# Local attention and a bilinear GLU in one kernel: products over finished q, k rows, tile sums on ScalarE

## The chip, the cores and the metric

The kernel runs on one core of a Trainium2 chip. The metric is the device time of one execution in microseconds (us); smaller is better. A core has a matrix engine (TensorE, PE in the profile), a vector engine (VectorE, DVE), a scalar engine (ScalarE, ACT), a general engine (GpSimd, POOL), a queue engine that here only starts transfers (SyncE, SP), and 16 DMA engines that move the data. Each engine takes its own instructions strictly in order; they meet through semaphores.

## The reference

```python
x = A_x                                   # 1 x 2048 x 640, bf16
xn = layernorm(x)                         # (x - mean) / sqrt(var + 1e-5)
q, k, v = split(xn @ wqkv)                # 32 heads of 20
idx = pos[:, None] - arange(8) * 2        # 8 window positions, 2 apart, back in time
logits = einsum("bhsd,bhswd->bhsw", q, k[idx]) * 20 ** -0.5     # idx < 0: -1e9
o = einsum("bhsw,bhswd->bhsd", softmax(logits), v[idx])
h = (xn @ w_gate) * (xn @ w_up)           # 640 -> 1536; the input B_x is not used
out = x + o @ wo + h @ w_down
```

The two branches read the same normalized xn, and their sum is added to x.

## The kernel before

The 2048 positions are 16 tiles of 128 (`t`), in four chunks of 512 (`c`, tiles 4c to 4c+3). A chunk goes through these stages:

- **Layer norm** (`ln`), by tile, on x with positions on partitions. For every tile DVE takes `bn_stats` of two halves (L251), aggregates (L257) and adds epsilon (L259); POOL raises to -1/2 (`rstd`, L265). Tiles 0-7 are then applied by DVE (L270); for tiles 8-15 POOL makes a shift (`ns`, L312) and ACT applies (L315).
- **Transposes** into `xnT` (channels on partitions): by PE for tiles 0-3, by DMA transposes on SP's queue for the others (L353). `xnT` has two buffers, one a chunk.
- **q, k, v** by PE (`qk` L419, `vproj` L452) into a ring of six PSUM banks; ACT copies every result out (L426, L458). POOL's queue stores v to DRAM (`vD`, L473), and SP loads it back as a window of eight shifted copies for each tile (`load_v8`, L613, 1280 KB).
- **Logits** (`products`, `fold`, `logits`). With channels on partitions, DVE multiplies q by shifted k (L520): eight instructions a chunk, each for two window positions and half a chunk, in five blocks of channels (`KT` = 5). Four tiles `("pw", c, u)` hold them. `fold` adds blocks together (L496); `LEVELS` says how far: chunk 0 leaves three blocks, chunk 1 two, chunks 2 and 3 one. PE sums over channels with a 0/1 matrix `Ek` (L539), four matmuls for each block that is left, in two groups `g` a chunk. ACT copies the logits out (L555), a DMA transpose on SP makes positions partitions (LT, L562).
- **Softmax** on DVE in two blocks for each half chunk (`mx` L581-585, `nrm` L598-603), Exp on ACT between them (L590).
- **Attention** (`av`), by tile: DVE multiplies the window by the weights (L638), adds up in a tree (L647, L651, L653) to `o`; SP transposes o to `oT` (L660, four buffers).
- **GLU** (`glu`): PE in 24 groups a chunk (L680), ACT copies out (L685), DVE multiplies to `hT` (L696).
- **Down** (`down`): for each tile PE sums hT by w_down (L740) and oT by wo (L743); ACT copies to `y` (L755); POOL's queue adds y to the output in DRAM (L784), which was seeded with x. The last two tiles go by DVE and SP.

One pool tag `pv` with five buffers holds both the products' tiles and the window loads, so that a window load can wait for PE's logits, and a product for an attention tile.

The order of the work on every engine is made by a planner in the kernel (`Plan`): every step has an engine, a cost, an occupation and dependencies; it is emitted by its planned start, the most urgent first. Emission order is the order on each engine. The planner knows the dependencies that are given to `add`; a buffer's reuse that isn't given is still waited for on the chip. An ACT or DVE step that follows another of its own engine is taken as ready when that one's occupation ends. The logits are urgent in PE's order (`LL[n].urgent`), and take a margin. `ring` gives the PSUM banks: a PE group waits for the copy that is six groups back.

Of the kernel before, what the change touches and what calls it, by code (L numbers as in the profile page):

```python
# [31 lines left out]
class Plan:  # L32


    LAG = 0.06
    INORDER = ("DVE", "PE", "ACT")
# [4 lines left out]
    def add(self, eng, cost, fn, deps=(), occ=None, after=(), kb=0):  # L41
        s = Step(eng, cost, fn, deps, occ, after)
        s.kb = kb
        s.idx = len(self.steps)
        self.steps.append(s)
        return s

    def order(self):
# [16 lines left out]
        while True:  # L65
            best = None
            for eng, items in ready.items():
                if not items:
                    continue
                f = free.get(eng, 0.0)  # L70
                t0 = max(f, min(r for r, _ in items))
                r, s = min((x for x in items if x[0] <= t0 + 1e-9), key=lambda x: (x[1].late, x[1].idx))
                if best is None or t0 < best[0]:
                    best = (t0, r, s)
# [10 lines left out]
            for t in s.succ:  # L85
                t.left -= 1
                if t.left == 0:
                    at = max(
                        d.start + d.occ if d in t.after else (d.start + d.occ if d.eng == t.eng and d.eng in self.INORDER else d.end + (0.0 if d.eng == t.eng else self.LAG) + t.margin)
                        for d in t.deps  # L90
                    )
                    ready.setdefault(t.eng, []).append((at, t))
# [5 lines left out]
def kernel(  # L98
# [17 lines left out]
    H = 32  # L116
# [182 lines left out]

    def ln(t):  # L300
        turn = [XT.get(t - (1 if t == CH else 2)), GL.get(t - 1)] if t < 2 * CH else []
        a = add("DVE", 0.48, ln_stats(t, 0), [X[t], GL.get(t - 3), *turn], occ=0.395)
        a = add("DVE", 0.48, ln_stats(t, 1), [a], occ=0.395)
        a = GL[t] = add("DVE", 0.39, ln_aggr(t), [a], occ=0.3)
        b = RS[t] = add("POOL", 0.56, ln_rstd(t), [a])
# [4 lines left out]
        def shift():  # L310
            ns = new(("ns", t), [P, 1], F32, "ns", 6)
            nc.gpsimd.tensor_scalar(ns[:], T["mv", t][:, 0:1], scalar1=T["rstd", t][:], scalar2=-1.0, op0=ALU.mult, op1=ALU.mult)  # L312
# [82 lines left out]
    Q, Kk, LASTPW = {}, {}, {}  # L395
    HALOCP = {}

    def halo(c):
# [8 lines left out]
        else:  # L407
            HALOCP[c] = add("ACT", 0.25, fn, [LASTPW.get(c - 2), *Kk[c - 1]])

    def qk(c, lo, n, rs=(0, 1)):  # L410
        for r in rs:
            for j in range(KT):
# [17 lines left out]
                mine = [WK if r else WQ, *[TX.get(t, TT[t]) for t in ts], LASTPW.get(c - 2)]  # L430
# [50 lines left out]
    PW, LL, LE, SS, DD, AA, O16, OE, V8, DT = {}, {}, {}, {}, {}, {}, {}, {}, {}, {}  # L481

    LEVELS = (1, 2, 3, 3)
    FOLDER = ('DVE', 'DVE', 'DVE', 'DVE')
    LEFT = (tuple(range(KT)), (0, 1, KT - 1), (0, KT - 1), (0,))
    HALVES = ((0, 2, 2, 4), (0, 1, 1, 2), (0, 1, KT - 1, KT))

    HS = CS // 2

    def fold(c, u):  # L490
        s = PW[8 * c + 2 * u + 1]
        for lo, hi, a, b in HALVES[: LEVELS[c]]:
            def fn(lo=lo, hi=hi, a=a, b=b):
                w = T["pw", c, u]
                if FOLDER[c] == "DVE":
                    nc.vector.tensor_tensor(w[:, :, lo:hi, :], w[:, :, lo:hi, :], w[:, :, a:b, :], ALU.add)  # L496
                else:
                    nc.gpsimd.dma_start(out=w[:, :, lo:hi, :], in_=w[:, :, a:b, :], accum_op=ALU.add)
            n = (hi - lo) * 4 * HS
            if FOLDER[c] == "DVE":  # L500
                s = add("DVE", 0.25 + n / 1920, fn, [s], occ=0.1 + n / 1920)
            else:
                s = add("POOL", 6.2, fn, [s], occ=1.2)
        return s

    def products(c, hf):
        for j in range(4):
# [15 lines left out]
            w = [LL.get(2 * c - 1), O16.get(4 * c - 4), O16.get(4 * c - 3), O16.get(4 * c - 2)][u]  # L523
            PW[m] = add("DVE", 1.48, mul, [*Q[c], *Kk[c], w], occ=1.395, after=[(FO[4 * c + 1] if i == 4 else PW.get(m - 1)) if i else V8.get(4 * c - 1)])
            if j % 2:
                FO[4 * c + u] = fold(c, u)
        LASTPW[c] = PW[m]

    PAIRED = ()

    def logits(c, g):
        n = 2 * c + g

        def lg():
            l = new(("lps", c, g), [P, 512], F32, "pl", 2, psum)
            left = LEFT[LEVELS[c]]
            for i in left:
                for j in range(4):
                    nc.tensor.matmul(l[H * j : H * (j + 1), :], lhsT=Ek[:], rhs=T["pw", c, 2 * g + j // 2][:, 2 * (j % 2) : 2 * (j % 2) + 2, i, :],  # L539
                                     start=(i == left[0]), stop=(i == left[-1]), tile_position=(0, H * j),  # L540
                                     skip_group_check=True)

        alone = not (g and c in PAIRED)
        took = 0.022 + 0.2195 * len(LEFT[LEVELS[c]]) + (0.19 if alone else 0.0)
# [30 lines left out]
    def softmax(c, hf):  # L575
        n = 2 * c + hf

        def mx():
            L4 = T["LT", n]
            m = sb.tile([P, 2, 4, H], BF, name="m", tag="m", bufs=1)  # L580
            nc.vector.tensor_tensor(m[:], L4[:, :, 0:4, :], L4[:, :, 4:8, :], ALU.max)  # L581
            nc.vector.tensor_tensor(m[:, :, 0:2, :], m[:, :, 0:2, :], m[:, :, 2:4, :], ALU.max)
            nc.vector.tensor_tensor(m[:, :, 0:1, :], m[:, :, 0:1, :], m[:, :, 1:2, :], ALU.max)
            d = new(("d", n), [P, 2, W, H], F32, "d", 2)
            nc.vector.tensor_tensor(d[:], L4[:], m[:, :, 0:1, :].to_broadcast([P, 2, W, H]), ALU.subtract)

        DD[n] = add("DVE", 1.52, mx, [SS[n], AA.get(n - 2)], occ=1.43)
# [7 lines left out]
        def nrm():  # L595
            d = T["d", n]
            s = sb.tile([P, 2, 4, H], F32, name="s", tag="s", bufs=1)
            nc.vector.tensor_tensor(s[:], d[:, :, 0:4, :], d[:, :, 4:8, :], ALU.add)  # L598
            nc.vector.tensor_tensor(s[:, :, 0:2, :], s[:, :, 0:2, :], s[:, :, 2:4, :], ALU.add)
            nc.vector.tensor_tensor(s[:, :, 0:1, :], s[:, :, 0:1, :], s[:, :, 1:2, :], ALU.add)  # L600
            nc.vector.reciprocal(s[:, :, 0, :], s[:, :, 0, :])
            a = new(("a", n), [P, 2, W, H], BF, "a", 2)
            nc.vector.tensor_tensor(a[:], d[:], s[:, :, 0:1, :].to_broadcast([P, 2, W, H]), ALU.mult)

        AA[n] = add("DVE", 2.33, nrm, [e, O16.get(2 * n - 3)], occ=2.24)

    def load_v8(t):
        def fn():
            v = new(("v8", t), [P, W, D], BF, "pv", 5)
# [21 lines left out]
    def av(t):  # L631
# [17 lines left out]
        def tree2():  # L649
            v = T["v8", t]  # L650
            nc.vector.tensor_tensor(v[:, 0:2, :], v[:, 0:2, :], v[:, 2:4, :], ALU.add)  # L651
            o = new(("o", t), [P, D], BF, "o", 2)
# [5 lines left out]
        def tr():  # L658
            o = new(("oT", t), [P, KT, P], BF, "oT", 4)
            nc.sync.dma_start_transpose(out=o[:], in_=T["o", t][:])  # L660
# [249 lines left out]
```

## Time and profile before

| | us |
|---|---|
| three runs: median (lowest, highest) | 261.53 (261.37, 263.31) |
| the profiled execution | 261.25 |
| its span, first to last instruction | 259.5 |
| busy: PE, DVE, ACT, POOL | 252.8, 230.4, 121.7, 48.5 |

The span is shorter than the time by what lies before the first and after the last instruction. The granted clock of the matrix engine is 1.00 throughout. DVE begins chunk 0's products at 23.2 us, and PE is at chunk 0's GLU from 42 to 68, at its down projections to 87, at chunk 2's q, k, v to 104, chunk 1's GLU to 131, its down projections to 149, chunk 3's q, k, v to 167, chunk 2's GLU to 193 and so on. In the answers about single instructions, a line has its start, the time it took (for `xN`, N instructions merged), engine, line of the kernel, operation, out<-in, shapes, and in brackets how long the engine idled before it and what released it. For transfers the time is that of the issue; the time to landing stands in a list of its own.

### The profile page before, as it was taken

To read this page: it belongs to the slowest core of one execution; us is meant where nothing else is said; L and a number is where in the kernel's file an instruction comes from. 1 tells how busy PE (TensorE), PEld (TensorE's weight loads), DVE (VectorE), ACT (ScalarE), POOL (GpSimd) and SP (SyncE) were. 2 spreads that over 40 slices of the span, in tenths; PEclk is the share of its full clock that TensorE was granted. 3 is DMA by queue.
4 is the path that set the end of the run, shared out by engine and by line. 5 is a ranking of instruction groups with operands and counts; after the bars stand their busy time and mean duration, and the time that the engine had idled before them with its cause. 6 is when DMAs were issued, how large, how long until landed. Compare 5 with 4: busy or idle time off the path is not lost.

```text
span 259.5 us, 3922 instructions
## 1 busy us (share of the span) xinstructions
PE 252.8 (97%) x1451; PEld 141.7 (55%) x1470; DVE 230.4 (89%) x336; ACT 121.7 (47%) x233; POOL 48.5 (19%) x85
## 2 busy tenths in 40 slices
PE   7999999999999999999999989999999999999995
PEld 2655554444676646444467745644457754445763
DVE  5684998999999999799999995999999976999961
ACT  2757566856321457675521156465541136654100
POOL 4552004201042115800222110200031120000110
PEclk9999999999999999999999999999999999999999
DMA  7989994999989604991168925971157236951251
GB/s 219 344 176 237 399 376 125 418 334 247 294 161 254 109 20 130 361 265 27 25 150 155 206 34 155 371 240 25 25 144 207 31 31 148 370 177 24 28 78 51
DMA packets 51507, 46.54 MB, mean 179 GB/s; under 512 B 24626, under 2 KB 49472, under 8 KB 51424
## 3 DMA queue, kind: packets, MB, share of 16 engines
q1 hardware_dynamic: 46704, 37.10, 49.9%
q0 software_dynamic: 3184, 8.05, 15.2%
q10 hardware_dynamic: 1600, 1.15, 1.4%
q8 instruction: 11, 0.18, 0.3%
q14 instruction: 8, 0.07, 0.1%
HBM read 35.39 MB, written 7.55 MB: 165 GB/s over the span
## 4 chain that ended last, share of the span: by engine, by line
PE 54%; DVE 39%; issue 2%; POOL 2%; DMA 1%; ACT 1%; DVEq 0%; ACTq 0%; POOLq 0%
PE ps L680 20%; PE ps L419 11%; PE ps L740 10%; DVE pv L520 9%; DVE pv L638 7%; PE ps L452 6%; DVE pv L496 6%; PE ps L743 4%; DVE pv L647 4%; DVE hT L696 3%; DVE pv L651 2%; PE ps L242 2%; POOL ns L312 1%; DVE st L251 1%; DMA LT<-L 1%
## 5 line engine op out<-in xcount | busy, mean ns | idle before, releaser
L680 PE MATMUL ps<-xnT,wg 128*128 128x512 bf16 x230 | 59.1, 379 | 0.9 <-ACT v_t L458 0.4
L680 PE MATMUL ps<-xnT,wu 128*128 128x512 bf16 x238 | 59.5, 379 | 0.1
L740 PE MATMUL ps<-wd,hT 128*128 128x320 bf16 (+2 forms) x383 | 57.3, 299 | 0.1
L520 DVE TENSOR_TENSOR pv<-q,k 128x2560 bf16<-128x2560 bf16 x32 | 46.0, 1485 | 3.4 <-ACT k L426 3.4
L740 PEld LDWEIGHTS <-hT 128*128 128x128 bf16 x384 | 37.2, 98 | 15.8
L638 DVE TENSOR_TENSOR pv<-pv,a 128x5120 bf16<-128x5120 bf16 x16 | 45.1, 2819 | 0.1
L680 PEld LDWEIGHTS <-wu 128*128 128x128 bf16 x240 | 23.5, 98 | 28.3
L680 PEld LDWEIGHTS <-wg 128*128 128x128 bf16 x240 | 23.2, 98 | 28.7 <-issue 1.6
L685 ACT CAST us<-ps 128x512 bf16<-128x512 f32 x48 | 28.3, 590 | 18.1 <-PE ps L680 17.1
L685 ACT CAST gs<-ps 128x512 bf16<-128x512 f32 x48 | 28.3, 589 | 17.9 <-PE ps L680 17.8
L755 ACT COPY y<-ps 128x320 f32<-128x320 f32 x28 | 11.5, 426 | 53.0 <-PE ps L743 32.5
L496 DVE TENSOR_TENSOR pv<-pv 128x1024 bf16<-128x1024 bf16 (+1 forms) x36 | 31.7, 922 | 0.3
L743 PE MATMUL ps<-wo,oT 128*128 128x320 bf16 (+2 forms) x160 | 27.0, 299 | 0.3 <-DMA oT<-o 0.3
L784 POOL DMA_DIRECT2D out_dram<-y x14 | 12.3, 878 | 78.6 <-ACT y L755 78.6
L647 DVE TENSOR_TENSOR pv<-pv 128x2560 bf16<-128x2560 bf16 x16 | 23.8, 1486 | 0.1
L452 PE MATMUL ps<-wv,xnT 128*128 128x320 bf16 x160 | 23.3, 300 | 0.4 <-ACT xnT L365 0.4
L696 DVE TENSOR_TENSOR hT<-gs,us 128x512 bf16<-128x512 bf16 x48 | 19.6, 418 | 3.8 <-ACT us L685 3.8
L419 PE MATMUL ps<-xnT,wk 128*128 128x512 bf16 x98 | 22.6, 380 | 0.1
L419 PE MATMUL ps<-xnT,wq 128*128 128x512 bf16 x96 | 22.2, 379 | 0.2
L452 PEld LDWEIGHTS <-xnT 128*128 128x128 bf16 x160 | 15.3, 98 | 7.4 <-ACT xnT L365 0.6
L743 PEld LDWEIGHTS <-oT 128*128 128x128 bf16 x160 | 15.4, 98 | 6.9 <-DMA oT<-o 0.7
L419 PEld LDWEIGHTS <-wk 128*128 128x128 bf16 x100 | 11.5, 118 | 10.3 <-issue 1.1
(60 smaller groups left out, 198.2 us busy)
## 6 DMA issues: line engine op xcount, KB each, us to landing
pv<-vD SPq DMA_DIRECT2D x16, 1280.0 KB, 9.1
vD<-v_t POOLq DMA_DIRECT2D x16, 160.0 KB, 5.2
out_dram<-y POOLq DMA_DIRECT2D x14, 160.0 KB, 3.8
wg<-in_B_w_gate_dram SPq DMA_DIRECT2D x1, 1920.0 KB, 7.7
wu<-in_B_w_up_dram SPq DMA_DIRECT2D x1, 1920.0 KB, 12.0
wd<-in_B_w_down_dram SPq DMA_DIRECT2D x1, 1920.0 KB, 12.3
out_dram<-in_A_x_dram POOLq DMA_DIRECT2D x3, 640.0 KB, 6.5
x<-in_A_x_dram SPq DMA_DIRECT2D x11, 160.0 KB, 5.7
```

What stands on the lines that cost most here:

```text
L419: nc.tensor.matmul(T[key][:, 0:n], lhsT=(wk if r else wq)[:, i, :].rearrange("p (c b) -> p c b", b=KT)[:, :, j], rhs=T["xnT", c][:, i, lo ...
L452: nc.tensor.matmul(T["psv", t, n][:, 0:NS], lhsT=T["xnT", c][:, i, q * P : (q + 1) * P], rhs=wv[:, i, n * NS : (n + 1) * NS], start=(i == ...
L496: nc.vector.tensor_tensor(w[:, :, lo:hi, :], w[:, :, lo:hi, :], w[:, :, a:b, :], ALU.add)
L520: nc.vector.tensor_tensor(o, qh, kh, ALU.mult)
L638: nc.vector.tensor_tensor(v[:].rearrange("p w (j h) -> p w j h", j=Dh, h=H), v[:].rearrange("p w (j h) -> p w j h", j=Dh, h=H), T["a", n][ ...
L647: nc.vector.tensor_tensor(v[:, 0:4, :], v[:, 0:4, :], v[:, 4:8, :], ALU.add)
L680: nc.tensor.matmul(ps[:], lhsT=(wu if r else wg)[:, i, f * P : (f + 1) * P], rhs=T["xnT", c][:, i, :], start=(i == 0), stop=(i == KT - 1))
L685: nc.scalar.copy(s[:], T[key][:])
L696: nc.vector.tensor_tensor(h[:], T["gs", c, f][:], T["us", c, f][:], ALU.mult)
L740: nc.tensor.matmul(ps, lhsT=T["hT", c, f][:, q * P : (q + 1) * P], rhs=wd[:, f, sl], start=(f == 0), stop=(f == FT - 1 and not wo_part))
L743: nc.tensor.matmul(ps, lhsT=T["oT", t][:, g, :], rhs=wo[:, g, sl], start=False, stop=(g == KT - 1 and f1 == FT))
L784: nc.gpsimd.dma_start(out=out_flat[t * P : (t + 1) * P, :], in_=T["y", t][:], accum_op=ALU.add)
```

## The change

1. **Products.** Chunk 0 is folded one level and leaves three blocks, as before. Chunks 1-3 are folded three levels to one block (`LEVELS` 1, 2, 3, 3 becomes in effect 1, 3, 3, 3); the last fold writes over rows 0-3 of `k` or `q` of that half chunk, whose products are then done, so that the `pw` tile is free for the next products. `pw` gets two buffers of its own and the window loads three (`v8`); chunk 0's second half borrows two of these. A product in chunks 1-3 waits for the fold two tiles back, and no more for logits or attention.
2. **Softmax** steps are planned one instruction at a time, and the last tree step of attention too; `o` is a step of its own. The planner adds 0.116 us between dependent DVE steps, and lets a more urgent step that is ready within 0.12 us go ahead of a long one.
3. **Layer norm of tiles 8-15**: ACT sums x (Identity with an accumulator), POOL scales to minus the mean (`nm`), ACT sums the squares of x + nm, POOL makes variance plus epsilon (`ve`), `rstd` and the shift (`ns`), and ACT applies as before. Three ACT passes a tile in place of one, four POOL operations in place of two, none on DVE.
4. **Logits** of chunks 2 and 3 are given as a pair: both groups wait for all four folds. Margins are 0.9 for chunk 0 and 2 for the others.
5. **Window loads** wait for the attention tile three back, and a chunk's first for the oT transpose before it. `oT` goes from four buffers to three.

The core of the diff:

```diff
@@ ln @@
+    ST_ACT = (8, 9, 10, 11, 12, 13, 14, 15)
+    def ln_sum(t):
+            nc.scalar.activation(T["x", t][:], T["x", t][:], ACT.Identity, accum_out=sm[:])
+    def ln_mean(t):
+            nc.gpsimd.tensor_scalar(nm[:], T["sm", t][:], scalar1=-1.0 / D, scalar2=None, op0=ALU.mult)
+    def ln_square(t):
+            nc.scalar.activation(sq[:], T["x", t][:], ACT.Square, bias=T["nm", t][:], accum_out=ss[:])
+    def ln_rstd_sq(t):
+            nc.gpsimd.tensor_scalar(ve[:], T["ss", t][:], scalar1=1.0 / D, scalar2=EPS, op0=ALU.mult, op1=ALU.add)
+            nc.gpsimd.tensor_tensor(rs[:], ve[:], mhalf[:], ALU.pow)
...
+        if t in ST_ACT:
+            a = GL[t] = add("ACT", 0.8, ln_sum(t), [X[t]], occ=0.7)
+            a = add("POOL", 0.3, ln_mean(t), [a])
+            a = add("ACT", 0.8, ln_square(t), [a], occ=0.7)
+            b = RS[t] = add("POOL", 0.9, ln_rstd_sq(t), [a])
...
+                nc.gpsimd.tensor_tensor(ns[:], T["nm", t][:], T["rstd", t][:], ALU.mult)
@@ fold, products @@
+    FIRST = 1
+    def summed(c, u):
+        if c == 0:
+            return [T["pw", 0, u][:, :, i, :] for i in LEFT]
+        lo = (u // 2) * HS
+        return [T["k" if u % 2 == 0 else "q", c][:, 0:4, lo : lo + HS]]
...
+        def last():
+            w = T["pw", c, u]
+            nc.vector.tensor_tensor(summed(c, u)[0], w[:, :, 0, :], w[:, :, KT - 1, :], ALU.add)
+        s = add("DVE", 1.22, level(0, 2, 2, 4), [s], occ=1.14)
+        if c == 0 and FIRST == 1:
+            return s
+        s = add("DVE", 0.69, level(0, 1, 1, 2), [s], occ=0.61)
+        if c == 0:
+            return s
+        return add("DVE", 0.69, last, [s, PW[8 * c + 4 * (u // 2) + 3]], occ=0.61)
...
-                    new(("pw", c, u), [P, 4, KT, HS], BF, "pv", 5)
+                    new(("pw", c, u), [P, 4, KT, HS], BF, *(("v8", 3) if c == 0 and hf else ("pw", 2)))
...
-            w = [LL.get(2 * c - 1), O16.get(4 * c - 4), O16.get(4 * c - 3), O16.get(4 * c - 2)][u]
+            w = None if c == 0 else LL[0] if c == 1 and hf == 0 else FO[4 * c + u - 2]
...
-    PAIRED = ()
+    PAIRED = (2, 3)
-        LL[n].margin = 0.9 if alone else 0.0
+        LL[n].margin = (0.9 if c == 0 else 2) if alone else 0.0
@@ load_v8 @@
-            v = new(("v8", t), [P, W, D], BF, "pv", 5)
+            v = new(("v8", t), [P, W, D], BF, "v8", 3)
...
-        order = [SPLAST[0]] if t < CH - 1 else [SS[2 * (t // CH) + 1]] if t % CH in (1, 2) else []
-        c, u = divmod(t, CH)
-        order.append(V8[t - 1] if u else PW[8 * c + 6])
+        order = [SPLAST[0]] if t < CH - 1 else []
+        if t:
+            order.append(V8[t - 1])
+        else:
+            order.append(PW[6])
...
+        if t >= CH and t % CH == 0:
+            order.append(OE[t - 1])
-        w = LL[2 * c + (u - 1) // 2] if u else O16.get(t - 1)
+        w = LL[1] if t in (1, 2) else O16.get(t - 3)
@@ av @@
-            o = new(("oT", t), [P, KT, P], BF, "oT", 4)
+            o = new(("oT", t), [P, KT, P], BF, "oT", 3)
-        O16[t] = add("DVE", 1.35, tree2, [b, OE.get(t - 2)], occ=1.26)
-        OE[t] = add("SP", 2.8, tr, [O16[t], DT.get(t - 4)], occ=1.3, kb=200, after=[V8[2]])
+        b = add("DVE", 0.82, tree2, [b], occ=0.74)
+        O16[t] = add("DVE", 0.49, tree3, [b, OE.get(t - 2)], occ=0.41)
+        OE[t] = add("SP", 2.8, tr, [O16[t], DT.get(t - 3)], occ=1.3, kb=200, after=[V8[2]])
```

`DT[t]` is PE's down projection of tile t. `attention(c)` is built before `down` of the same chunk, so that `DT.get(7 - 3)` finds nothing when the step of tile 7's transpose is built.

Not shown: the planner's two small rules and the softmax steps, which run the same operations as before, one to a step. In SP's built order, chunk 1's three oT transposes of tiles 5-7 now stand ahead of the window loads of tiles 8-10, and these ahead of the four xnT transposes of tiles 12-15.

More of the change, by code (lines that the diff above doesn't have):

```diff
@@ L46, in add, with after_end @@
         return s
+    def after_end(self, d, t):
+        if d in t.after:
+            return d.start + d.occ
+        if d.eng == t.eng and d.eng in self.INORDER:
+            return d.start + d.occ + (self.RAW if d.eng == "DVE" else 0.0)
+        return d.end + (0.0 if d.eng == t.eng else self.LAG) + t.margin
     def order(self):
@@ L72, in order @@
                 r, s = min((x for x in items if x[0] <= t0 + 1e-9), key=lambda x: (x[1].late, x[1].idx))
+                if eng == "DVE" and s.occ > 0.6:
+                    near = min((x for x in items if x[0] <= t0 + 0.12), key=lambda x: (x[1].late, x[1].idx))
+                    if near[1] is not s:
+                        r, s = near
+                        t0 = max(f, r)
                 if best is None or t0 < best[0]:
@@ L87, in order @@
                 if t.left == 0:
[L88 to L91, printed above, removed]
+                    at = max(self.after_end(d, t) for d in t.deps)
                     ready.setdefault(t.eng, []).append((at, t))
@@ L522, in products @@
             m = 8 * c + i
[L523 to L529 removed]
+            w = None if c == 0 else LL[0] if c == 1 and hf == 0 else FO[4 * c + u - 2]
+            PW[m] = add("DVE", 1.48, mul, [*Q[c], *Kk[c], w], occ=1.395, after=[PW.get(m - 1)])
+        for u in (2 * hf, 2 * hf + 1):
+            FO[4 * c + u] = fold(c, u)
+    PAIRED = (2, 3)
     def logits(c, g):
```

118 lines of the change are left out of this document (68 added, 50 removed).

## The prediction

> **What bounds the kernel now.** I read the page's busy times first, then what TensorE (PE) waited for, then PE, POOL and SyncE (SP) in order of time.
>
> ```profile
> span 259.5 us, 3922 instructions
> PE 252.8 (97%) x1451; PEld 141.7 (55%) x1470; DVE 230.4 (89%) x336; ACT 121.7 (47%) x233; POOL 48.5 (19%) x85
> ```
>
> PE is busy 97% at full granted clock. A faster VectorE (DVE) alone therefore buys almost nothing; only PE's own work and waits count.
>
> ```profile
> PE ps L242 <- DVE wv L192: 1.3, 1, 1.3
> PE pl L539 <- DVE pv L496: 0.6, 1, 0.6
> PE ps L680 <- ACT v_t L458: 0.4, 1, 0.4
> PE ps L452 <- ACT xnT L365: 0.4, 1, 0.4
> PE ps L743 <- DMA oT<-o: 0.3, 1, 0.3
> ```
>
> Columns: total, times, longest. The start (1.3, 0.4) is untouched by the change. The other three, 0.63 + 0.40 + 0.34 in the timeline, are all that can be won back.
>
> PE in order of time, around chunk 1's logits and before chunk 3's q, k:
>
> ```profile
> 93.20 0.62 PE L539 MATMUL pl<-pv,Ek 128*32 128x512 bf16 x8
> 93.75 3.43 PE L419 MATMUL ps<-xnT,wk 128*128 128x512 bf16 x14
> ...
> 134.06 0.84 PE L743 MATMUL ps<-wo,oT 128*128 128x320 bf16 x5
> ...
> 149.14 3.40 PE L419 MATMUL ps<-xnT,wq 128*128 128x512 bf16 x14
> ```
>
> From start to next start, eight logits matmuls hold PE 0.55 us (93.20 to 93.75), four 0.33 (153.17 to 153.50, chunk 2). At 134.74 PE is through with oT of tile 4; at 149.14 it begins chunk 3's q, k.
>
> POOL beside DVE:
>
> ```profile
> 96.91 0.26 POOL L312 TENSOR_SCALAR ns<-mv,rstd 128x1 f32<-128x1 f32 x1
> ...
> 103.19 2.87 POOL L312 TENSOR_SCALAR ns<-mv,rstd 128x1 f32<-128x1 f32 x1
> ```
>
> ```profile
> 103.10 2.83 DVE L638 TENSOR_TENSOR pv<-pv,a 128x5120 bf16<-128x5120 bf16 x1
> 105.96 1.49 DVE L647 TENSOR_TENSOR pv<-pv 128x2560 bf16<-128x2560 bf16 x1
> ```
>
> The same 128x1 operation takes 0.26 us alone and 2.87 when it begins just after a DVE multiply: it ends when the multiply does (the next, at 106.03, took 1.55 and ended with the tree add). So a POOL operation under DVE's two-input stream costs about one DVE operation.
>
> SP's queue, and landings of what it issued at 101.7 and 108.87:
>
> ```profile
> 100.46 2.36 SPq L613 DMA_DIRECT2D pv<-vD  x3
> 108.87 20.07 SPq L660 DMA_TRANSPOSE oT<-o  x3
> 130.86 4.75 SPq L353 DMA_TRANSPOSE xnT<-x  x2
> 135.70 1.23 SPq L660 DMA_TRANSPOSE oT<-o  x1
> 137.02 3.06 SPq L353 DMA_TRANSPOSE xnT<-x  x2
> ```
>
> ```profile
> pv<-vD SPq DMA_DIRECT2D x1, 1280.0 KB, 15.0
> ```
>
> ```profile
> oT<-o SPq DMA_TRANSPOSE x1, 8.6
> ```
>
> The third window load landed at 101.7 + 15.0 = 116.7; the transpose issued at 108.87 landed at 117.5, right behind it, where a lone one takes 2.6. What SP issues lands in order. Chunk 3's four xnT transposes were all issued by 140.1, ahead of chunk 2's window loads (the first at 140.18, the rest at 158.36).
>
> The profiled execution took 261.25 us (span 259.5 and 1.7 around it), 0.28 below the median of three runs, 261.53. The sum is made against 261.25, and 0.28 added at the end.
>
> **PE's own work.** Chunk 1 drops from two summed blocks to one: 2 x (0.55 - 0.33) = 0.44 us saved. Pairing: in the built order chunk 2's two groups are still split by five q matmuls (nothing saved); chunk 3's stand together: 2 x 0.33 plus a gap of 0.10 becomes 0.55, 0.21 saved. With the three waits taken out, 261.25 - 0.65 - 1.37 = 259.23. That is a floor; waits that the change makes come on top.
>
> **DVE.** Eight tiles lose two statistics (0.40 each from start to start), an aggregate (0.20) and an addition (0.15): 9.2 us. Chunk 1 gains four 1024-element folds of 0.68: 2.7. About 6.5 us less of DVE lies beside PE: worth 0. The single softmax steps interleave the same operations, and the products' own slots free DVE to do four of chunk 1's products early: also 0, as DVE had no wait on a slot.
>
> **Layer norm on ScalarE (ACT) and POOL.** Two new ACT passes a tile: between 0.63 (Exp of 512) and 0.92 us (L315, 640 elements); I take 0.75, 12 us in all, 47 to 52% busy, hidden unless they wait. They do: POOL's four small operations a tile stand between them, and ACT is in order. The Trainium skill ("ScalarE: Activation LUTs", What ACT_TABLE_LOAD costs) gives 186 ns + 0.833 ns per element, so 0.72 for the sum; by it nothing changes.
>
> Tiles 9-11 fall under chunk 0's products and folds, which keep DVE full from 23.2 to 41.9 (1.40 us a product, 1.14 a fold, from the k copy's end at 23.2). ACT reaches the square of tile 9 at 34.5, behind k copies and sums, and ends it at 35.2. Then POOL's operations end with DVE's: 35.3 (ve 9), 36.7 (rstd 9), 37.9 (ns 9), 39.0 (ve 10), 40.5 and half a microsecond of its own (rstd 10). Behind them on POOL stands the vD store of tile 4: 41.0 instead of 36.85. Behind the last apply (its ns ends near 43.0) stand on ACT the copy of chunk 0's second logits, v of tile 7, the first gs and us, and the first Exp, near 47.3. So the first attention multiply starts at 51.2, where DVE's order alone, summed from 23.2, puts it at 49.1: a lag of 2.1 us (1.1 if nothing is held, from the wait for the first LT; 5.1 if each rstd takes two DVE operations). PE itself loses nothing here: six PSUM banks, 1.08 us a group, cover it.
>
> Tiles 13-15 come during chunk 0's down projections: 13 POOL operations under DVE's attention, folds and products from 76 to 92 (0.6 to 1.4 us each). ACT's order is y2, sum, apply 13, y3, sum, two squares, y4, apply 14, y5. Counted the same way from the landing of tile 13's x near 76, copy y5 ends at 91.6 with a DVE lag of 0, at 94.8 with 5.1, so near 92.9 with 2.1. PE needs y5's bank for its fourth q group of chunk 2: 86.63 + 3 x 1.08 - 0.34 + 0.33 (the first logits group now stands ahead) + gaps, 89.9. **Stall 3.0 us** (0 if POOL is not held; 5.2 with the later DVE and the other copies behind). oT of tiles 1 and 2, which follow DVE's order and so come 1 to 2 us late for PE, are covered by this stall: PE waits earlier instead. So is tile 8's load: issued on ACT at 11.89, 3.8 to landing, it holds ACT's first sum and the q copies behind it from 13.4 to 15.7; the banks cover that (0, at most 0.7 if tile 7's transpose slips past 23.8, where q of chunk 1 begins).
>
> **SP's queue.** oT falls from four buffers to three. The built order makes oT of tile 7 wait for PE's last use of tile 4's; the plan has no such edge, since tile 4's projection is planned later. Behind it on SP stand three window loads (tiles 8-10, formerly slot-bound to after the logits), then all four xnT transposes of chunk 3. Times: 134.74 - 0.34 - 0.40 - 0.44 + 3.0 = 136.6 for the release; 1.2 for the transpose; loads from 137.8. Three such loads took 16.2, 15.0 and 13.8 us from first issue to last landing (issues at 100.46, 158.36, 217.52); I take 15.0, the middle: 152.8. Then four transposes: 0.8 behind, as at 117.5, and three times 0.75 (what a lone one keeps the DMA engines busy): 155.8. PE wants chunk 3's q at 149.14 - 1.18 + 3.0 + 0.33 = 151.3: **stall 4.5 us**, with v and all GLU queued behind it. Ends: 13.8 + 0.8 gives 1.1; 16.2 + 0.8 + 3 x 1.25 (issue spacing) gives 7.2. The Trainium skill ("DMA: Bandwidth & Descriptors", Bandwidth) has about 358 GB/s for HBM per core; 3.93 MB would then take 11 us, the stall 0.5 and the sum 263.0 on the runs' scale; the rows are slower, and I keep them.
>
> Chunk 3's loads stand behind oT of tile 11 in the same way, but what follows them is LT, not xnT: some 2 us late for DVE, which then has 32 us of work and is wanted by PE only with the last oT, 40 us on (0). The other window loads come well ahead in three slots of their own (0).
>
> **Sum:** 259.23 + 3.0 + 4.5 = 266.73; with 0.28, **267.0 us**, 2.1% over 261.53.
>
> **Rivals.**
> (1) Not slower: the transposes pass the window loads, at SP's queue near 138. Then 259.23 + 3.0 + 0.28 = 262.5, +0.4%. It decides from a stall under 1.6 us. The landing of 8.6 us at 108.87 speaks against it.
> (2) POOL's operations slip between DVE's: no bank stall, 259.23 + 4.5 + 0.28 = 264.0. For it: 0.56 us for rstd at 96.24; but DVE ran statistics there.
> (3) Neither stall, the change does what its words say: 259.5. PE is at its bound, so there is no more to gain.
> (4) POOL holds DVE as well. If each of about 12 small operations in chunk 0 (0.26 to 0.56 us) stopped DVE, some 3 us, the bank stall would go to 5.2: 269.2. Against it: the tree add at 105.96 followed its multiply at the usual 0.03 us, with POOL waiting. The Trainium skill has this rule ("SBUF — State Buffer", Who interferes with whom): whichever of the two starts first has the shared port pair for its whole instruction. The half in which DVE is first agrees with the 2.87 us.
>
> **How the numbers follow.** Forecast 0.66 (own range 264.1 to 270), rivals 0.10, 0.12, 0.06, 0.06. Range 262.3 to 270.0: it takes in (1), (2), (4) and leaves out (3) and the far ends, both stalls at most being 259.23 + 5.2 + 7.2 + 0.28 = 271.9. One per cent is about what a measurement of this kernel can tell from no change: 258.9 to 264.1. Faster 0.02 (under the floor); same 0.22: (1), (3), half of (2); slower 0.76.
>
> **What would show it.** PE waiting 3 to 6 us for an xnT transpose at its first q group of chunk 3, with SP's oT of tile 7 ending after PE's tile 4; PE waiting some 3 us on ACT's y near its fourth q group of chunk 2; POOL operations of 1 to 3 us at 31-42 and 76-92; logits groups of four in chunk 1. I am wrong if xnT lands before 152, or the small POOL operations stay at 0.3 to 0.6.

## The result: slower by about 5%, and the profile after

The changed kernel took 275.1 to 285.2 us in the first four runs (median 279.6) and 274.6 to 278.3 in four more on another chip (median 277.5), against medians of 261.45 and 262.3 for the kernel before. The ratio is 1.052 [1.045, 1.059] and 1.057 [1.050, 1.063]. Forecast were 267.0 us and 262.3 to 270.0: slower was right, the size was not. The first profiled execution (283.65 us) was one of the longer ones, so the rows below are from one of 274.6 us, the same kernel under the label `again`; further down, the profiles of oT4, LT, LTeoT4, befL3 and allP8 are of executions 3.0 to 5.4 us over the lowest of their kernel.

The page's busy times of the changed kernel:

```profile
span 272.9 us, 3931 instructions
PE 255.6 (94%) x1462; PEld 141.2 (52%) x1462; DVE 222.9 (82%) x308; ACT 131.7 (48%) x265; POOL 59.5 (22%) x101
```

DVE lost 7.5 us (6.5 were forecast), ACT gained 10.0 (12 were). PE has 2.8 us more of busy time, though it does less work, and 17.3 us of idle time where it had 6.7. What PE waited for (total, times, longest):

```profile
PE ps L469 <- DMA xnT<-x: 7.8, 1, 7.8
PE ps L820 <- DMA oT<-o: 2.3, 2, 2.1
PE ps L817 <- DVE hT L773: 1.4, 3, 0.7
...
PE ps L469 <- ACT y L832: 1.0, 1, 1.0
```

The same waits in order of time on PE:

```profile
81.81 0.85 PE L820 MATMUL ps<-wo,oT 128*128 128x320 bf16 x5 [2.12 <-DMA oT<-o]
...
94.28 1.02 PE L469 MATMUL ps<-xnT,wq 128*128 128x512 bf16 x4 [1.01 <-ACT y L832]
...
160.47 2.30 PE L469 MATMUL ps<-xnT,wq 128*128 128x512 bf16 x5 [7.83 <-DMA xnT<-x]
```

Three numbers hold the loss. From chunk 0's first down projection to chunk 1's first GLU group, PE takes 40.2 us instead of 36.6 (below: stretch A). From chunk 1's first down projection to chunk 2's first GLU group it takes 45.7 instead of 36.3 (stretch B). From chunk 2's first down projection to the end of the span it takes 67.7 instead of 66.6 (C). The GLU stretches between give back 0.6, and the start is the same: 3.6 + 9.3 + 1.1 - 0.6 = 13.4, which is the difference of the spans.

In B the wait of 7.83 is not all. Answers by stretch (start and end, length; then the busy time of PE, PEld, DVE, ACT and POOL, each with its number of instructions):

```profile
160.00:163.00 3.00, 2.53 (x9) 0.71 (x9) 1.40 (x4) 0.19 (x1) 0.00 (x0) 0.50 0.02 6
163.00:169.00 6.00, 6.00 (x27) 2.82 (x24) 1.64 (x5) 3.52 (x7) 0.00 (x0) 0.82 0.11 22
169.00:180.00 11.00, 11.00 (x68) 6.84 (x67) 10.73 (x12) 7.12 (x15) 1.67 (x3) 1.00 0.19 50
```

The last three columns are the granted clock, the DMA share and GB/s. After the long idle PE starts again at half the clock: five q matmuls take 2.30 us where five of the same shape take 1.24. The 25 q matmuls took 7.5 us instead of 5.4 (k's 25 right after them), so 2.1 more: most of PE's extra busy time. SP's queue ahead of that wait, and what DVE waited for:

```profile
139.24 4.04 SPq L682 DMA_DIRECT2D v<-vD  x3
143.33 14.21 SPq L403 DMA_TRANSPOSE xnT<-x  x4
157.63 7.54 SPq L620 DMA_TRANSPOSE LT<-L  x2
```

```profile
DVE m L645 <- DMA LT<-L: 23.2, 5, 8.0
```

Three window loads go out from 139.24 on, right behind the oT transpose of tile 7, which waited for PE's last use of tile 4's oT (over at 137.75). The third lands near 156.4, the last xnT transpose at 160.2. LT stands behind both. In the kernel before DVE waited for LT 4.8 us in all, here 23.2.

### The profile page after: what moved, and what is told of

Read it like the earlier page. It is cut to its first block, busy times and chain, and to the rows that moved or that the text cites. A ratio compares the mean times of both kernels' runs of the same rounds, so it can differ in the third digit from the quotient of the medians.

```text
span 281.9 us, 3912 instructions
## 1 busy us (share of the span) xinstructions
PE 257.7 (91%) x1443; PEld 141.5 (50%) x1462; DVE 222.9 (79%) x308; ACT 130.0 (46%) x265; POOL 63.1 (22%) x101
## 4 chain that ended last, share of the span: by engine, by line
PE 38%; DVE 21%; DMA 14%; POOL 8%; SPq 7%; issue 6%; ACT 5%; POOLq 0%; ACTq 0%; DVEq 0%
PE ps L757 17%; PE ps L817 9%; DVE v L711 7%; SPq L403 6%; DMA x<-in_A_x_dram 5%; DMA LT<-L 5%; PE ps L469 5%; DMA xnT<-x 4%; DVE v L720 4%; PE ps L820 3%; POOL nm L321 3%; PE ps L502 3%; DVE hT L773 3%; POOL rstd L336 2%; DVE pw L579 1%
## 5 line engine op out<-in xcount | busy, mean ns | idle before, releaser
L817 PE MATMUL ps<-wd,hT 128*128 128x320 bf16 (+2 forms) x383 | 59.5, 304 | 3.2 <-DVE hT L773 3.0
L817 PEld LDWEIGHTS <-hT 128*128 128x128 bf16 x384 | 37.3, 99 | 21.7 <-DVE hT L773 4.7
L711 DVE TENSOR_TENSOR v<-v,a 128x5120 bf16<-128x5120 bf16 x16 | 45.1, 2821 | 1.3 <-DMA v<-vD 1.2
L579 DVE TENSOR_TENSOR pw<-q,k 128x2560 bf16<-128x2560 bf16 x28 | 40.7, 1486 | 4.0 <-ACT k L476 3.9
L469 PE MATMUL ps<-xnT,wq 128*128 128x512 bf16 x96 | 24.6, 408 | 8.4 <-DMA xnT<-x 7.8
L645 DVE TENSOR_TENSOR m<-LT 128x256 bf16<-128x256 bf16 x8 | 2.3, 291 | 30.4 <-DMA LT<-L 30.4
L550 DVE TENSOR_TENSOR pw<-pw 128x2048 bf16<-128x2048 bf16 (+1 forms) x26 | 24.7, 974 | 0.2
L720 DVE TENSOR_TENSOR v<-v 128x2560 bf16<-128x2560 bf16 x16 | 23.8, 1486 | 0.1
L469 PEld LDWEIGHTS <-wq 128*128 128x128 bf16 x100 | 11.8, 121 | 19.8 <-issue 11.3
```

The lines of the kernel that those rows point to most:

```text
L469: nc.tensor.matmul(T[key][:, 0:n], lhsT=(wk if r else wq)[:, i, :].rearrange("p (c b) -> p c b", b=KT)[:, :, j], rhs=T["xnT", c][:, i, lo ...
L579: nc.vector.tensor_tensor(o, qh, kh, ALU.mult)
L711: nc.vector.tensor_tensor(v[:].rearrange("p w (j h) -> p w j h", j=Dh, h=H), v[:].rearrange("p w (j h) -> p w j h", j=Dh, h=H), T["a", n][ ...
L720: nc.vector.tensor_tensor(v[:, 0:4, :], v[:, 0:4, :], v[:, 4:8, :], ALU.add)
L817: nc.tensor.matmul(ps, lhsT=T["hT", c, f][:, q * P : (q + 1) * P], rhs=wd[:, f, sl], start=(f == 0), stop=(f == FT - 1 and not wo_part))
```

## The experiments

Time is the lowest of the runs; the ratio is to the kernel before on the same chip. A, B and C are the stretches above, from the profiled execution. xnTfirst and oT4 leave the order on PE, DVE and ACT as it was; with most of the other edits the planner sets it anew in places, so that a ratio is that of an edit with its order, and a cause is read from the waits.

| run | lowest us | ratio, 95% | A | B | C |
|---|---|---|---|---|---|
| before | 260.8 | 1 | 36.6 | 36.3 | 66.6 |
| again (the changed kernel) | 274.6 | 1.057 [1.050, 1.063] | 40.2 | 45.7 | 67.7 |
| xnTfirst | 269.3 | 1.033 [1.025, 1.041] | 40.3 | 37.7 | 70.4 |
| oT4 | 267.4 | 1.025 [1.018, 1.031] | 41.0 | 41.3 | 66.5 |
| xLst0 | 273.4 | 1.044 [1.040, 1.049] | 40.3 | 39.4 | 72.4 |
| LT | 270.0 | 1.040 [1.034, 1.045] | 43.0 | 36.7 | 68.6 |
| LTe | 266.7 | 1.022 [1.019, 1.025] | 41.1 | 36.0 | 68.5 |
| LTeoT4 | 265.8 | 1.018 [1.015, 1.022] | 43.3 | 36.1 | 68.9 |
| LTe8 | 266.0 | 1.018 [1.015, 1.021] | 42.5 | 35.4 | 68.3 |
| tm | 278.9 | 1.072 [1.067, 1.078] | 44.2 | 46.3 | 68.0 |
| LTetm | 265.0 | 1.018 [1.014, 1.021] | 41.0 | 36.0 | 67.0 |
| LTe0tm | 263.4 | 1.010 [1.008, 1.011] | 35.6 | 37.8 | 69.2 |
| befST | 269.6 | 1.032 [1.030, 1.034] | 45.0 | 35.9 | 66.6 |
| befL3 | 262.9 | 1.008 [1.005, 1.012] | 37.1 | 36.9 | 67.6 |
| LTe8tm | 261.8 | 1.002 [1.000, 1.004] | 38.7 | 35.4 | 67.2 |
| LTe0tmP | 260.8 | 0.997 [0.996, 0.999] | 35.6 | 37.3 | 66.6 |
| LTetmA | 259.2 | 0.994 [0.992, 0.996] | 35.6 | 35.9 | 67.1 |
| allP8 | 261.6 | 1.003 [1.001, 1.005] | 39.8 | 35.6 | 67.2 |
| LTeA_P | 259.2 | 0.997 [0.994, 1.000] | 35.6 | 35.6 | 66.7 |

**again.** 

> The changed kernel as it is, for a profile and a time to set the others against. Both theories: 275 us, 1.05 of the kernel before, with PE's wait for an xnT transpose of 6 to 8 us at chunk 3's q.

Measured as expected; it is the profile shown above.

**xnTfirst and oT4: stretch B.**

```diff
 # xnTfirst, load_v8
-            order.append(OE[t - 1])
+            order += [OE[t - 1], *([TT[u] for u in (12, 13, 14, 15)] if t == 8 else [])]
...
 # oT4, ln_square (whose activation also takes saturate=False) and av
-            sq = new(("sq", t), [P, D], BF, "sq", 1)
+            sq = new(("sq", t), [P, D], mybir.dt.float8e4, "sq", 1)
...
-            o = new(("oT", t), [P, KT, P], BF, "oT", 3)
+            o = new(("oT", t), [P, KT, P], BF, "oT", 4)
```

> Three oT buffers as in the changed kernel, but the xnT transposes of tiles 12 to 15 stand ahead of the window loads of tiles 8 to 10 in SP's queue; orders on PE, ACT and POOL unchanged. Theory A: the transpose of tile 7 still waits for PE's tile 4, but then four transposes of about 1.2 us follow, so that xnT lands some 10 us before PE wants it; PE's wait goes, chunk 3's LT stays late: 267 to 269 us. Theory C (the loads are then as much later, and what they hold comes back): PE's wait moves to hT or oT of chunk 2, 273 to 276 us.

> Four oT buffers instead of three, no other order of work on any engine (the squares' output, which nothing reads, is stored in one byte to make room). Theory A (three oT buffers let SP's transposes of tiles 7 and 11 wait for PE's projections, and all that stands behind them starts late): the window loads start some 12 us earlier in both places, PE's wait at chunk 3's q goes and so does the late LT of chunk 3: 264 to 267 us. Theory B (three window loads ahead of the xnT transposes in the queue are enough): the transposes still land late for PE, 272 to 275 us.

The transposes ahead of the loads remove 8.0 of B's 9.3 us; the fourth buffer removes 4.4 in the profiled execution and, by the ratios, 3.2% of the whole. Both times lie at the upper end of theory A's ranges or just over it. So the release by PE's tile 4 and the order behind it both have a part in the stall. Theory B of oT4 (the three loads are enough) fails by the time; but in its profiled execution the loads left 1.0 us after chunk 1's first down projection instead of 5.6, so 4.6 us earlier and not 12, and PE still waits 3.6 us for xnT: there the order alone makes a stall, a smaller one. No profile shows the faster executions of oT4. And xnTfirst gives 2.7 us back in C (70.4 against 67.7), as theory C said in kind. The loads now stand between xnT and LT, and DVE idles 8 us for LT. That this makes the folds of chunk 3 late, for which PE waits 1.8 us in C (at 217.6), was not tried by itself:

```profile
163.05 0.29 DVE L645 TENSOR_TENSOR m<-LT 128x256 bf16<-128x256 bf16 x1 [7.95 <-DMA LT<-L]
```

```profile
PE pl L598 <- DVE k L555: 3.1, 2, 1.8
```

**xLst0: all that the forecast had named, undone at once.** As xnTfirst, with LT ahead of the loads in chunk 3 and `ST_ACT = ()`.

> xnT transposes ahead of the window loads, chunk 3's two LT transposes ahead of the loads of tiles 13 and 14, and the statistics of tiles 8 to 15 on DVE as in the kernel before (the new products, softmax steps and pairing stay). Theory A (the three places are the whole loss): 259 to 262 us. Theory D (the new order of DVE and PE loses by itself): 264 to 268 us.

273.4 us: theory D's side, and worse than it. Stretch A stays at 40.3 with no statistics on ACT at all. PE still waits 3.3 us for the oT of tile 2 there, and in B 3.2 for a copy y. DVE idles 6.5 and 9.4 us for LT in chunks 1 and 2, where the loads still stand ahead of it. My theory of the loss was therefore incomplete. Two causes had to be looked for: the loads ahead of LT in chunks 1 and 2 too, and what makes oT of chunk 0 late.

**LT, LTe, LTeoT4, LTe8: the loads' rule of the kernel before put back.**

```diff
 # LT, load_v8 (all that follow have this too)
-        w = LL[1] if t in (1, 2) else O16.get(t - 3)
+        order += [SS[2 * (t // CH) + 1]] if t >= CH and t % CH in (1, 2) else []; w = LL[1] if t in (1, 2) else O16.get(t - 3)
...
 # LTe: also, softmax and ln
-        e = add("ACT", 0.635, ex, [DD[n]], occ=0.54)
+        e = T["exp", n] = add("ACT", 0.635, ex, [DD[n]], occ=0.54)
...
-        XT[t] = add("ACT", 0.78, apply, [b], occ=0.7)
+        XT[t] = add("ACT", 0.78, apply, [b], occ=0.7, after=[T["exp", 0]] if t in (9, 10, 11) else [])
 # LTeoT4: LTe with the edit of oT4;  LTe8: LTe with
+    ST_ACT = (8, 9, 10, 11)
```

> The changed kernel, with one rule of the kernel before put back: in chunks 1 to 3 the window loads of a chunk's second and third tile stand behind both its LT transposes in SP's queue; so only one load stands ahead of xnT and LT. Three oT buffers stay. Theory E (the loss from chunk 1's logits on is LT and xnT landing behind three loads): DVE's waits for LT fall from 23 to under 8 us, PE's wait at chunk 3's q goes, what stays is the 3.6 us between chunk 0's down projections and chunk 1's GLU: 264 to 266 us. Theory F (the loads then come late for attention): DVE waits for window loads instead, and PE for oT and hT: 268 to 273 us.

> As the run before, and chunk 0's first Exp stands on ACT ahead of the layer norm applies of tiles 9 to 11. Theory E with G (chunk 0's oT comes late because that Exp, at 47.5 us where the kernel before has it at 43.6, stands behind applies that wait for POOL): first attention multiply 2 to 3 us earlier, PE's wait for oT of 2.1 us and most of the wait for y go: 261 to 263 us. Theory H (the copy y behind POOL's operations holds PE anyway, as forecast for the fourth q group): the oT wait goes, a wait for y of 2 to 3 us takes its place: 264 to 266 us.

> As the run before with four oT buffers. Theory E with G: nothing more to gain, within 1 us of the run before. Theory A (three oT buffers cost by themselves): 2 to 5 us under the run before.

> As the second run of this set, but tiles 12 to 15 take their statistics on DVE, as in the kernel before; tiles 8 to 11 on ACT and POOL. Theory H: the wait for y goes: 261 to 263 us. Theory G: DVE has 4.6 us more to do in chunk 0's attention and the oT of tiles 1 to 3 come later again: 1 to 3 us over the second run.

B is mended by this one rule, 36.7 and 36.0 us, with three oT buffers; a fourth adds nothing beyond 0.9 us (LTeoT4). So theory E holds for B: PE's wait at chunk 3's q is gone. But DVE still waits 15.6 us for LT in the run LT and 10.8 in LTe, where E had under 8. Of theory F the reason fails (DVE waits 1.5 us in all for window loads), though the run LT, 270.0 us, lies in its range. Neither E's total nor G's came out, because A did not shrink. In LTe the first attention multiply starts at 50.3 instead of 51.6, yet PE waits longer for oT, and the clock falls again (0.65 from 82 to 86 us):

```profile
82.29 0.85 PE L820 MATMUL ps<-wo,oT 128*128 128x320 bf16 x5 [3.42 <-DMA oT<-o]
```

```profile
82.00:86.00 4.00, 3.71 (x18) 2.27 (x19) 3.93 (x5) 3.44 (x9) 2.95 (x5) 0.65 1.01 297
```

LTe8 shows the same wait (3.0), and xLst0, with no statistics on ACT, 3.3. So neither the Exp nor ACT's statistics explain the late oT. The order of DVE in the changed kernel (`again`) does:

```profile
66.04 0.82 DVE L724 TENSOR_TENSOR v<-v 128x1280 bf16<-128x1280 bf16 x1
66.78 0.42 DVE L773 TENSOR_TENSOR hT<-gs,us 128x512 bf16<-128x512 bf16 x1
67.11 2.82 DVE L711 TENSOR_TENSOR v<-v,a 128x5120 bf16<-128x5120 bf16 x1
69.85 0.48 DVE L729 TENSOR_TENSOR o<-v 128x640 bf16<-128x640 bf16 x1
...
73.73 2.83 DVE L711 TENSOR_TENSOR v<-v,a 128x5120 bf16<-128x5120 bf16 x1 [0.59 <-DMA v<-vD]
76.48 0.48 DVE L729 TENSOR_TENSOR o<-v 128x640 bf16<-128x640 bf16 x1
```

Tile 1's last tree step (L729), a step of its own since the change, stands behind tile 2's multiply (L711), and tile 2's behind tile 3's. The likely reason is the 0.116 us that the planner now adds between dependent DVE steps, by which the multiply is ready first; that was not tried alone. o of tile 1 comes at 69.85 where the kernel before has it at 64.9; o of tile 2, for whose oT PE waits, at 76.48 where it was 71.3.

**tm and LTetm: the last two tree steps as one again.**

```diff
-        b = add("DVE", 0.82, tree2, [b], occ=0.74)
-        O16[t] = add("DVE", 0.49, tree3, [b, OE.get(t - 2)], occ=0.41)
+        both = lambda: (tree2(), tree3())
+        O16[t] = add("DVE", 1.35, both, [b, OE.get(t - 2)], occ=1.26)
 # tm: this alone;  LTetm: with LTe
```

> The changed kernel with the last two tree steps of attention planned as one step again, as in the kernel before; all else as changed. Theory I (the last tree step, alone, was planned behind the next tile's multiply of 2.8 us, so that o and oT of tiles 1 and 2 come about 3 us late): PE's wait of 2.1 us for oT in chunk 0's projections goes, the xnT wait of chunk 3 stays: 271 to 273 us. Theory G (it is only the late first Exp): PE's wait for oT stays near 2 us, 274 to 276 us.

> LT ahead of the window loads, chunk 0's first Exp ahead of the applies, the last tree steps as one: all that stands out so far undone, while the one-block products, their own slots, the statistics on ACT and the pairing stay. Theory J (these three places are the whole loss): PE's waits for oT of 3.4 and 1.4 us in the run with the first two go, with a fall of the clock behind the first: 260 to 262 us. Theory D (the new products, slots and statistics lose more by themselves): 263 to 266 us.

In both the waits for oT in chunk 0's projections are gone, and in tm o of tiles 1 and 2 comes at 64.5 and 73.4: theory I is right in its mechanism. But tm, 278.9 us, is 4 us slower than the changed kernel, outside both ranges, and A grows to 44.2. What the late oT had covered comes out in its place, at chunk 2's fourth q group, where the forecast had put it. tm, then LTetm:

```profile
95.27 4.43 PE L469 MATMUL ps<-xnT,wq 128*128 128x512 bf16 x10 [4.21 <-ACT y L832]
```

```profile
93.36 4.01 PE L469 MATMUL ps<-xnT,wq 128*128 128x512 bf16 x10 [2.70 <-ACT y L832]
```

Ten such matmuls take 2.35 us at the full clock, so the clock costs 2.1 and 1.7 us on top of each wait in these ten alone; in tm the next ten took 3.19, 0.8 more. Theory J fails; 265.0 us lies in D's range, for a reason that D did not name.

**LTe0tm, befST, LTe8tm: is it the statistics on ACT and POOL?** LTe0tm is LTetm with `ST_ACT = ()`, LTe8tm with `ST_ACT = (8, 9, 10, 11)`. befST is the kernel before with the new `ln` and its helpers alone, four oT buffers and `sq` in one byte.

> As the run before, with the statistics of all tiles on DVE. Theory J: ACT and POOL are no loss by themselves once nothing urgent stands behind them; DVE has 9 us more to do, beside PE: the same within 1 us, or 1 to 2 us slower by late oT. Theory K (POOL beside DVE costs by itself): 1 to 3 us faster than the run before.

> The kernel before with the third part of the change alone: the sums of tiles 8 to 15 on ACT and POOL (the squares' output in one byte, to keep four oT buffers). Theory H (the copy y stands behind POOL's small operations for tiles 13 to 15 and holds a PSUM bank that chunk 2's q needs, as forecast): PE waits 2 us or more for y there, with a fall of the clock behind it: 264 to 267 us. Theory L (only the new order of DVE brings POOL into the way): no wait for y, 260.5 to 262.5 us.

> LT ahead of the loads, chunk 0's first Exp ahead of the applies, the last tree steps as one, and only tiles 8 to 11 on ACT and POOL; tiles 12 to 15 on DVE. Theory H: the wait for y of 2.7 us goes: 261 to 263.5 us. Theory M (it is the POOL operations of tiles 9 to 11 that set the later copies back): the wait for y stays over 1.5 us, 265 us or more.

Yes. Without them A is 35.6 us, under the kernel before, there is no wait for y, and the time is 1.5 us under LTetm's: theory K. With them alone, in the old order of everything else, A is 45.0 us: PE waits 0.99 and then

```profile
96.95 3.75 PE L459 MATMUL ps<-xnT,wq 128*128 128x512 bf16 x10 [4.41 <-ACT y L795]
```

The third part of the change, alone, costs 3.2%: theory H in kind, and over its 264 to 267 us. Tiles 12 to 15 make it: back on DVE, the wait for y goes (LTe8tm; its A is 38.7 by a late hT, 2.4 us).

**LTetmA: is it POOL's operations or ACT's passes?**

```diff
 # LTetm with three of POOL's four small operations a tile done by ACT (epst: a 128x1 tile of epsilon); the planner's entries are not shown
-            nc.gpsimd.tensor_scalar(nm[:], T["sm", t][:], scalar1=-1.0 / D, scalar2=None, op0=ALU.mult)
+            nc.scalar.activation(nm[:], T["sm", t][:], ACT.Identity, scale=-1.0 / D)
...
-            nc.gpsimd.tensor_scalar(ve[:], T["ss", t][:], scalar1=1.0 / D, scalar2=EPS, op0=ALU.mult, op1=ALU.add)
+            nc.scalar.activation(ve[:], T["ss", t][:], ACT.Identity, scale=1.0 / D, bias=epst[:])
...
-                nc.gpsimd.tensor_tensor(ns[:], T["nm", t][:], T["rstd", t][:], ALU.mult)
+                nc.scalar.activation(ns[:], T["nm", t][:], ACT.Identity, scale=T["rstd", t][:])
```

> LT ahead of the loads, Exp first, last tree steps as one, statistics of tiles 8 to 15 on ACT, and of POOL's four small operations a tile (minus the mean, variance plus epsilon, power, shift) three are done by ACT; only the power stays on POOL. Theory H in its narrow form (it is the number of POOL operations under DVE's stream, each held for a DVE instruction, that sets y back): with one instead of four a tile the wait for y of 2.7 us falls under 0.7 us, 261 to 263.5 us. Theory N (it is ACT's own passes and their order): the wait stays 2 us or more, 265 us or over.

259.2 us, 0.994 [0.992, 0.996]: theory H in its narrow form, below its range, and by the ratio the fastest kernel here. Tiles 13 to 15 on POOL in LTetm (four of 11 rows, from 79.3 to 93.2; an operation takes from 0.2 to 1.9 us), then all of them in LTetmA:

```profile
87.33 1.02 POOL L336 TENSOR_TENSOR rstd<-ve,mhalf 128x1 f32<-128x1 f32 x1
88.44 1.06 POOL L334 TENSOR_SCALAR ve<-ss 128x1 f32<-128x1 f32 x1
89.59 1.68 POOL L336 TENSOR_TENSOR rstd<-ve,mhalf 128x1 f32<-128x1 f32 x1
91.24 1.93 POOL L358 TENSOR_TENSOR ns<-nm,rstd 128x1 f32<-128x1 f32 x2
```

```profile
84.59 2.32 POOL L343 TENSOR_TENSOR rstd<-ve,mhalf 128x1 f32<-128x1 f32 x3 [0.23 <-ACT ve L336]
```

On ACT the 24 such operations of LTetmA take 0.20 to 0.37 us each, one of them here:

```profile
83.10 0.20 ACT L323 ACTIVATE nm<-sm 128x1 f32<-128x1 f32 x1
```

ACT makes the same passes over x in both (in an order that differs in places), so it was not their time. In LTetm ACT idled for ns, and the copies y4 and y5 stood behind the applies that need it:

```profile
92.07 0.92 ACT L365 ACTIVATE x<-x,ns,rstd 128x640 bf16<-128x640 bf16 x1 [4.14 <-POOL ns L358]
92.90 0.40 ACT L832 COPY y<-ps 128x320 f32<-128x320 f32 x1
```

**befL3, LTe0tmP, allP8, LTeA_P: the one-block fold and the pairing.** befL3 is the kernel before with `LEVELS = (1, 3, 3, 3)`. LTe0tmP and LTeA_P are LTe0tm and LTetmA with `PAIRED = ()`; allP8 is LTe8tm with it.

> The kernel before with chunk 1 folded to one block and nothing else (the fold levels 1, 3, 3, 3). Forecast: PE saves 0.44 us, DVE's 2.7 us more lie beside it: 260.6 to 261.4 us, 0.997 to 1.000. Theory D (DVE is too full for it): logits, hT or oT come late, 262 to 264 us.

> The fastest version so far (LT ahead of the loads, Exp first, last tree steps as one, all statistics on DVE), with the logits of chunks 2 and 3 not paired. If the pair costs (both groups wait for all four folds, so both LT come late and hT moves behind attention), PE's waits for hT of 3.8 us and for folds of 0.5 us shrink: 261 to 262.5 us. If it is the forecast's 0.2 us of PE work and no more: 263.4 to 263.9 us.

> LT ahead of the loads, Exp first, last tree steps as one, logits of chunks 2 and 3 not paired, and tiles 8 to 11 alone on ACT and POOL. If the statistics of tiles 8 to 11 are of use on ACT: 259.3 to 260.5 us. If they only delay chunk 0's attention: 261 to 262.5 us, over the version without them.

> The fastest version so far (LT ahead of the loads, Exp first, last tree steps as one, statistics on ACT with only the power on POOL), with the logits of chunks 2 and 3 not paired. If the pair costs as it did with the statistics on DVE (2.6 us): 258 to 259 us. If the wait for hT that the pair made there was due to DVE's fuller stream: within 0.7 us of 260.0 us.

The fold alone costs 0.8%: theory D. DVE's 2.7 us came right ahead of chunk 1's logits, and PE, with 0.4 us less to do, waited for it:

```profile
98.36 0.40 PE L539 MATMUL pl<-pv,Ek 128*32 128x512 bf16 x4 [1.24 <-DVE pv L496]
```

In the same profile PE also waits 1.9 us for a copy of v (0.4 before) and 1.5 for hT (none before); how the 0.8% is made up of these is not shown.

The pair costs 2.7 us where DVE is full (the lowest times of LTe0tm and LTe0tmP), most of it a wait of 2.28 us for a late hT within chunk 3's projections, which goes without it. Where DVE is free of the statistics the pair costs nothing that can be told (259.2 both, ratios 0.994 and 0.997 with overlapping intervals): the second case of LTeA_P. allP8, 261.6 us, is no better than LTe8tm and over LTe0tmP, which has no statistics on ACT: its second case.

## Why the prediction was wrong, point by point

- **The floor, 259.23 us.** Right as a floor: LTetmA and LTeA_P reach 259.2 once the stalls are gone, with A 1.0 and B 0.4 to 0.7 us under the kernel before.
- **"DVE ... lies beside PE: worth 0", "also 0, as DVE had no wait on a slot".** Wrong. What counted was not DVE's total but its order. The last tree step, planned alone, fell behind the next tile's multiply (5 us for the o of tiles 1 and 2). The fold put 2.7 us ahead of the logits that PE waits for (1.24 us in befL3). In LTetmA, which keeps the fold but not the lone tree step, PE waits only 0.6 us for DVE after the start: there "worth 0" holds.
- **Bank stall, 3.0 us at the fourth q group (0 to 5.2).** Place, cause and size right: 2.7 us in LTetm, 4.2 in tm, 5.4 in befST (in two groups, so over the upper bound by 0.2). In the changed kernel the oT of tile 2 takes 2.1 of it beforehand and y 1.0: the forecast said that PE would wait earlier instead, yet named 3 us on y as the sign. That POOL's operations under DVE set y back is what LTetmA confirms; that each costs one DVE operation is not a rule (below). Left out was the price after the wait: the clock, 2.9 us in tm, 1.7 in LTetm and 1.4 in befST.
- **xnT stall, 4.5 us (1.1 to 7.2).** This is the step that failed most. The mechanism was right (the release by tile 4, three loads, four transposes in order, PE at the first q group). The term was mis-sized, over its own upper bound: 7.83 us. The first load left at 139.2 instead of 137.8, the third landed 17.2 us after that instead of 15.0, the transposes 3.8 behind instead of 3.05: 160.2 instead of 155.8, against a PE that was there at 152.6 instead of 151.3. Why the loads took 17.2 us stays open: POOL's queue started four adds of y beside them (160 KB each), but four v stores of the same size ran beside two of the three rows that I took (16.2 and 15.0) and none beside the third (13.8). Then 2.1 us for the clock, in no term of the sum: 9.9 us instead of 4.5.
- **The clock.** No row of the kernel before shows it: its clock is 1.00 throughout, and PE's longest wait there after the start is 0.63 us. In the traces of the changed kernels half the clock was granted for 3.41 us or for two or three times that (LTetm from 93.5, 3.41 us; tm from 94.4, 6.83; `again` from 154.9, 10.24), so 3.41 us of it cost a busy PE 1.7 us of work. The Trainium skill has the rule ("TensorE: Matmul & The Clock Gate", What's actually happening): after an idle window of about 3.4 us the clock is halved, until PE has been busy for as long. The runs agree in kind: 0.50 after 7.83 us idle, and a fall with every wait of 3.3 us or more in the traces. But the length of a wait alone does not decide it: the clock fell after 2.70 us too (LTetm, 0.66 over the 5 us that follow) and after 1.95 (LTeoT4, 0.66), and not after 2.38 (LTe8tm) or 3.17 (xLst0). By the 1.4 to 2.9 us measured here, the forecast's own stall of 4.5 us would have cost about 2 us more (an estimate).
- **"The other window loads come well ahead ... (0)"; chunk 3's LT "some 2 us late for DVE", 0 for PE.** Wrong. DVE waited 4.2 us for LT in chunk 1, 6.4 and 4.3 in chunk 2, 8.0 in chunk 3. C grew by 1.1 us, with 0.9 of it in waits for hT; how much of that is LT's doing is not shown. The rule that kept LT ahead of the loads was removed by the change, and I costed the loads' slots, not what stands behind them in the queue.
- **Tiles 9-11, DVE lag 2.1 us, PE 0.** The lag at the first multiply was 3.05 (51.56 against 48.51), and PE lost nothing here in this execution. In others it lost 1.7 to 1.9 (below).
- **Rivals.** (1), transposes pass the loads, fails by the landings (156.4, then 160.2); (2), POOL slips between DVE's operations, by LTetm's rows; (3), neither stall, by both. (4), POOL holds DVE too: four products take 5.69 us in the changed kernel (84.34) with POOL's operations beside them from 85.5 on, and 5.69 in the kernel before (77.35), where POOL has none; DVE is not held there.

Against 261.25 the execution of 274.6 has 13.35 us more. The forecast's terms had 5.5. Of the missing 7.9, the mis-sized xnT wait has 3.3, the clock after it 2.1, the end 1.1. The rest, 1.4, is in A and the GLU stretches. This accounts for the execution of 274.6 us; the medians lie 2.9 and 5.0 us higher. The one profile of a longer execution (283.65) has 3.1 us more before chunk 0's down projections, 1.7 in A, 1.2 in B and 3.0 in C. Of the first, POOL's held operation (below) has 1.8; the rest stays open.

## What to carry to other kernels

When a change makes steps smaller or takes an ordering rule away, read the new order of each engine and queue for what is urgent and now stands behind something long. Engine totals tell nothing of it, and a wait that is removed can uncover the next (tm). Here small operations did better on an engine that nothing held up: three 128x1 operations a tile moved from POOL to ACT turned a version 1.8% over the kernel before into one 0.6% under it. A wait of PE of 2 us or more can cost up to 2.9 us again by the clock (tm): here every wait of 3.3 us or more brought a fall, and some from 1.95 us on did.

## What the runs showed of the hardware that was not expected

- **POOL can be held for a whole run of DVE operations, or not.** Tiles 9 to 11's three nm operations under chunk 0's products and folds (two inputs each), in `again` and in oT4, whose instructions are in the same order on every engine:

```profile
30.75 2.42 POOL L321 TENSOR_SCALAR nm<-sm 128x1 f32<-128x1 f32 x2 [5.45 <-ACT x L315]
33.97 0.34 POOL L321 TENSOR_SCALAR nm<-sm 128x1 f32<-128x1 f32 x1 [0.80 <-ACT x L315]
```

```profile
30.69 8.74 POOL L321 TENSOR_SCALAR nm<-sm 128x1 f32<-128x1 f32 x3 [5.45 <-ACT x L315]
```

  In the second the first of the three operations took 8.40 us by itself, the others 0.20 each, and POOL ends only as DVE's stream does (39.1 us); ACT's squares and a k copy wait behind it, and PE loses 1.66 us. The row is 7.5 to 8.7 us in LT, LTeoT4, allP8 and the first profiled execution of the changed kernel as well, where PE lost 1.7 to 1.9. What decides between the two was not tried. The forecast's bound of two DVE operations for one of POOL's was too low.
- **Issue on SP is held too.** The four xnT transposes took 14.2 us to issue behind three window loads (one of them 7.7), 5.4 when they stood ahead (xnTfirst).
- **An activation with an accumulator is two instructions**, 0.74 and 0.19 us for the sum, 0.84 and 0.20 for the squares (`again`); from start to start they take 0.73 and 0.83, so the second is nearly hidden.
